# A transformer layer's first stage: value weights loaded ahead of key weights, key weights folded once, 128-row products for the first two pairs of tiles, and a new order of issue

## The chip, the cores and the metric

One core of a Trainium2 chip runs the kernel. The metric is device time in microseconds; the kernel before took 389.91 (median of 3 runs, 389.55 to 390.11). A core has TensorE (PE; its weight loads are shown as PEld), VectorE (DVE), ScalarE (ACT) and GpSimd (POOL), and SyncE (SP), which here only issues transfers. Each takes its instructions in program order; between engines they wait on semaphores. Times inside the execution are from one profiled execution, in us from the start of its span.

## What is computed

2,048 rows of 576 numbers pass a pre-norm layer: linear attention with learned feature maps (32 heads of 18), then an MLP (576 to 4,608 to 576).

```python
x = A_x
y = layernorm(x)
q, k, v = split(y @ wqkv)                      # 32 heads of 18
pq, pk = q @ w_phi, k @ w_phi                  # per head, 18 x 18
phi_q = concat(softmax(pq), softmax(-pq))      # 36 features per head
phi_k = concat(softmax(pk), softmax(-pk))
kv, z = sum_s phi_k v, sum_s phi_k
o = (phi_q @ kv) / (phi_q @ z + 1e-6)
h = x + o @ wo
out = h + gelu(layernorm(h) @ w1 + b1) @ w2 + b2
```

## The kernel before

The 2,048 rows are 16 tiles of 128, worked on as 8 pairs `p` of two tiles. All activations and weights are bf16, products gather in PSUM in fp32.

**Stage one** needs every row before it ends, because `kv` and `z` are sums over all rows. First w_phi is multiplied into the key and query weights ("folding"), so that one product gives `pk` or `pq`. For the keys, the weights (`wk`) are loaded, turned on PE (`flip_mm`, 5 groups of heads, 25 transposes), copied out of PSUM (`flip_ev`), and multiplied by the block-diagonal w_phi `bd` (`fold_k_mm`) into nine blocks of rows `wkp`; `fold_k_ev` copies each block out. The query weights come turned by DMA (`turn_wq`), are folded into five blocks, and the other rows of `wqp` are filled by copies inside SBUF (`swap_q`).

Rows are normalised (`stats`, `power`, `centre`, `scale`) and turned, pair 0 on PE, the others by transposing DMAs on SP (`turn_dma`), into `turned(p)`: 9 blocks of 64 columns of each of the two tiles, tile 0 on partitions 0 to 63 and tile 1 on 64 to 127. A product (`value_mm`, `key_mm`, `query_mm`; line L450) of one pair and one half of the columns is therefore 18 matmuls of 64 rows, in nine couples of one for each tile, that run side by side on the two halves of the array; a pair takes two products, 36 matmuls. There are 16 products of each kind (8 pairs, two halves of 288 columns). ACT copies values out (`value_ev`, L460) and takes the exponentials of keys and queries (two activations each, L472); DVE sums and inverts (`key_sum`, L501 and L503); POOL, sometimes DVE, multiplies (`key_weigh`, L507; `query_weigh`, L536). `sums` (L586) adds a tile's 11 products into `acc_kv`.

Then `table` makes kvm from `acc_kv`, `combine_mm` and `divide` (L686, L687) give o of pair 0, `turn_o_mm` turns it, `residual_mm` (L722) multiplies by wo, DVE adds and normalises (`residual_add`, `second`, `rescale`), and `turn2_mm` turns the rows for **stage two**, the MLP: `up` (L1161, followed by gelu on ACT, L1183) and `down` (L1205), with the attention of later pairs between. Query products that are left fill PE while DVE works on this chain. `gelu_table` (L781) runs one gelu on four numbers ahead of time, so that ACT's table of functions is loaded early.

**Order.** Each engine's order is written out by hand, as one list of calls from `warm(13)` on. Transfers wait in SP's queue (a few in ACT's and POOL's) in the order of the list. PSUM has three tiles of two banks (`two`) for everything in stage one; each call takes the next in turn. After stage one the same banks become six of one bank each (`acc`).

## Time and profile before

| | |
|---|---|
| runs, median (lowest to highest) | 389.91 us (389.55 to 390.11) |
| the profiled execution's span | 391.7 us |
| first value product starts | 15.69 us |
| last of the sums over all rows ends | 66.96 us |
| first MLP product starts | 86.00 us |
| last MLP product ends | 389.03 us |
| weight loads on the chain ahead of the first PE work | 5.99 us |

The profile gives no time of its own for the profiled execution beside its span; the span is 1.8 us longer than the median of the runs. How to read its lines: busy time is the time in which an engine has an instruction running, so 98% on PE does not say that PE runs at its best; "idle" names what released the engine; "issue" is waiting for which the profile shows no cause. The chain of work is followed back from the last instruction to whatever released each step.

### The profile page before, as it was taken

How to read it: one execution, taken by the hardware profiler on the slowest of the kernel's cores; microseconds unless marked ns; L12 is line 12 of the kernel's file. 1: busy time of each engine (PE TensorE's matmuls, PEld its weight loads, DVE VectorE, ACT ScalarE, POOL GpSimd, SP SyncE). 2: the span in 40 equal slices, each digit the busy share in tenths (PEclk: the TensorE clock that was granted, in tenths of full speed). 3: DMA queues.
4: the chain of work that ended last, by engine and by line, in shares of the span. 5: the costliest groups of instructions: out<-in, count | busy, mean ns of one | idle time of the engine just before them, and what ended most of it. 6: DMA issues, size and time to landing. Idle time of an engine off the chain costs nothing.

```text
span 391.7 us, 10190 instructions
## 1 busy us (share of the span) xinstructions
PE 383.0 (98%) x4475; PEld 269.0 (69%) x4475; DVE 166.0 (42%) x364; ACT 163.2 (42%) x291; POOL 117.8 (30%) x161
## 2 busy tenths in 40 slices
PE   7999999799999999999999999999999999999997
PEld 3778779479978887844457887444677764447773
DVE  6998997385249388590019322000480000000100
ACT  2998995478500850046650000666300016661000
POOL 6399998116404654144003111000031110000120
PEclk9999999899999999999999999999999999999999
DMA  8977599999455578433003462000071000000000
GB/s 250 259 128 128 93 218 188 238 313 248 148 105 102 98 105 136 94 66 68 2 2 62 89 108 48 17 1 2 2 105 47 17 15 2 2 2 0 17 28 19
DMA packets 74096, 34.93 MB, mean 89 GB/s; under 512 B 61028, under 2 KB 71524, under 8 KB 74052
## 3 DMA queue, kind: packets, MB, share of 16 engines
q1 hardware_dynamic: 72944, 32.78, 40.3%
q0 software_dynamic: 336, 1.33, 1.2%
q8 instruction: 35, 0.57, 0.7%
q10 hardware_dynamic: 772, 0.17, 0.2%
q14 instruction: 9, 0.07, 0.1%
HBM read 16.47 MB, written 2.36 MB: 48 GB/s over the span
## 4 chain that ended last, share of the span: by engine, by line
PE 93%; ACT 2%; DMA 2%; issue 1%; DVE 1%; SPq 0%
PE po L1205 36%; PE ph L1161 36%; PE pk L450 8%; PE pv L450 5%; PE pa L722 4%; DMA w<-in_A_wqkv_dram 2%; PE acc_kv L586 1%; PE pn L673 1%; ACT home L472 1%; ACT shared L412 0%; DVE xh L731 0%; PE pW L419 0%; PE pW L405 0%; PE pT L359 0%; PE pX L377 0%
## 5 line engine op out<-in xcount | busy, mean ns | idle before, releaser
L1183 ACT ACTIVATE home<-ph,b1col 128x512 bf16<-128x512 f32 (+1 forms) x180 | 98.4, 598 | 169.1 <-PE ph L1161 165.9
L1205 PE MATMUL po<-w,home 128*128 128x288 bf16 (+2 forms) x1152 | 143.3, 286 | 0.0
L1161 PE MATMUL ph<-shared,w 64*128 64x512 bf16 (+2 forms) x1638 | 141.3, 331 | 0.6 <-ACT shared L364 0.6
L1205 PEld LDWEIGHTS <-home 128*128 128x128 bf16 x1152 | 109.4, 98 | 32.1 <-issue 1.8
L1161 PEld LDWEIGHTS <-w 64*128 64x128 bf16 x1638 | 80.3, 94 | 60.5 <-issue 0.7
L1209 DVE TENSOR_TENSOR ot<-po,hb 128x288 bf16<-128x288 f32 (+2 forms) x32 | 14.4, 453 | 106.4 <-PE po L1205 96.7
L450 PEld LDWEIGHTS <-home 64*128 64x128 bf16 x864 | 42.9, 95 | 13.6 <-issue 3.3
L1194 POOL TENSOR_TENSOR hb<-xh,b2bc 128x576 f32<-128x576 bf16 x16 | 20.4, 1273 | 104.6 <-DVE ot L1209 102.8
L536 POOL TENSOR_TENSOR padded<-home,rq 128x540 bf16<-128x540 bf16 x32 | 34.9, 1102 | 34.5 <-DVE rq L528 18.9
L731 DVE TENSOR_TENSOR xh<-pa,xh 128x288 bf16<-128x288 f32 x32 | 13.0, 447 | 72.4 <-PE pa L722 72.4
L274 POOL TENSOR_TENSOR rs<-va,mhalf 128x1 f32<-128x1 f32 x16 | 8.8, 549 | 110.9 <-DVE va L272 110.9
L507 POOL TENSOR_TENSOR phik<-phik,rk 128x576 bf16<-128x576 bf16 x28 | 33.4, 1218 | 1.4 <-DVE rk L503 1.2
L472 ACT ACTIVATE home<-pk 128x576 bf16<-128x576 f32 x32 | 18.6, 665 | 12.7 <-PE pk L450 10.4
L450 PE MATMUL pk<-wqp,home 64*128 64x288 bf16 x288 | 20.5, 293 | 2.8 <-issue 2.8
L501 DVE TENSOR_REDUCE sk<-phik 128x64 f32<-128x1152 bf16 x16 | 21.0, 1312 | 1.7 <-ACT phik L472 1.6
L527 DVE TENSOR_REDUCE sk<-home 128x64 f32<-128x1152 bf16 x16 | 21.0, 1310 | 0.0
L686 DVE RECIPROCAL rec<-pn 128x18 f32<-128x18 f32 (+1 forms) x32 | 8.0, 249 | 28.5 <-PE pn L673 28.5
L450 PE MATMUL pv<-wv,home 64*128 64x288 bf16 x288 | 19.6, 283 | 0.0
L472 ACT ACTIVATE phik<-pk 128x576 bf16<-128x576 f32 x32 | 18.7, 656 | 1.8 <-PE pk L450 1.1
L450 PE MATMUL pk<-shared,home 64*128 64x288 bf16 x288 | 19.3, 283 | 0.0
L722 PE MATMUL pa<-wo,shared 64*128 64x288 bf16 x288 | 18.6, 283 | 0.0
L722 PEld LDWEIGHTS <-shared 64*128 64x128 bf16 x288 | 13.9, 94 | 4.5 <-issue 0.5
(76 smaller groups left out, 208.3 us busy)
## 6 DMA issues: line engine op xcount, KB each, us to landing
w<-in_B_w_dram SPq DMA_DIRECT2D x21, 432.0 KB, 8.7
out_dram<-ot SPq DMA_DIRECT2D x15, 144.0 KB, 2.2
xh<-in_A_x_dram SPq DMA_DIRECT2D x3, 576.0 KB, 6.8
wo<-in_A_wo_dram SPq DMA_DIRECT2D x4, 324.0 KB, 8.0
w<-in_B_w_dram POOLq DMA_DIRECT2D x3, 432.0 KB, 13.0
wv<-in_A_wqkv_dram SPq DMA_DIRECT2D x2, 576.0 KB, 8.7
w<-in_A_wqkv_dram SPq DMA_DIRECT2D x1, 576.0 KB, 6.0
wqp<-wqp SPq DMA_DIRECT2D x2, 288.0 KB, 3.9
```

Source lines behind the costliest of these rows:

```text
L450: nc.tensor.matmul(dst[:, a, 0:HALF], lhs[rows, c, :], w[rows, slot, i * HALF : (i + 1) * HALF], start=(n == 0), stop=(n == KC - 1),)
L472: nc.scalar.activation(rows[:, :, i * HH : (i + 1) * HH, s, :], flight[key, p, i][:, :, 0:HALF].rearrange("p a (h f) -> p a h f", f=DH), A ...
L501: nc.vector.tensor_reduce(sk[:, :, :], part_of(dst, i), AX.X, ALU.add)
L507: eng.tensor_tensor(part, part, flight["r" + key, p, i][:, a, :].rearrange("p (h o) -> p h o", o=1).to_broadcast([P, NH, DH]), ALU.mult,)
L527: nc.vector.tensor_reduce(sk[:, :, :], part_of(phiq[p], i), AX.X, ALU.add)
L536: eng.tensor_tensor(padded[:, a, g0 * P : (g0 + 5) * P].rearrange("p (g k) -> p g k", k=P)[:, :, 0:STEP].rearrange("p g (h f) -> p g h f", ...
L722: nc.tensor.matmul(pa[a], oT[p % 2][rows, c, :], wo[rows, c, cs], start=(c == 0), stop=(c == KC - 1),)
L1161: nc.tensor.matmul(ph[half][:, lo:hi], w1[p_ // 9][rows, c, p_ % 9 * P : (p_ % 9 + 1) * P], ln2T[rows, c, base + lo : base + hi], start=(c ...
L1183: nc.scalar.activation(hidden(m), ph[half][:, 0:width], AF.Gelu_apprx_tanh, bias=b1col[:, m : m + 1], scale=1.0,)
L1194: nc.gpsimd.tensor_tensor(hb[:, :], xh[:, t, :], b2bc[:, :], ALU.add)
L1205: nc.tensor.matmul(po[:, :], hidden(m)[:, i_ * P : (i_ + 1) * P], w2[m // 18][:, m % 18, cs], start=(j == 0), stop=(j == NM - 1),)
L1209: nc.vector.tensor_tensor(ot[:, cs], po[:, :], hb[:, cs], ALU.add)
```

## The change

What it does, by parts:

- **Loads.** The value weights are loaded first, in five pieces; the key weights follow x's tiles 2 and 3. The last 64 rows of the key weights are loaded twice, into both halves of their block. x comes in smaller pieces; wo in two loads in place of four, since `divide` now writes o in an order that makes wo's rows contiguous. The second quarter of w1 is loaded piece by piece in the list, in place of six loads at `close_keys`.
- **Pairs 0 and 1** (`NAT = 2`) keep their rows as they are: `turn_n_mm` turns them on PE into 4 blocks of 128 columns and one of 64 for each tile. Their value, key and query products (`project_n`) are for each tile 8 matmuls of 128 rows and 2 of 64 rows (the "tail"). What follows goes by tiles, not by halves of the columns.
- **Key fold.** Five blocks of 128 rows in place of nine; the odd blocks, which the 64-row products of pairs 2 to 7 need, are copied inside SBUF by two DMAs (`swap_k`).
- **PSUM tiles** are named by number and taken from a list of free ones (`grab`, `give`), in place of pools that hand them out in turn.
- **Order.** The list is new from its first call to the MLP. The first products are pair 0's values.

```diff
-    wTk = borrowed(NG, D).rearrange("p (g f) -> p g f", g=NG)
+    wTk = borrowed(NG, DP).rearrange("p (g f) -> p g f", g=NG)
...
+    def grab(kind, key, shape, dt):
+        n = held[kind, key] = free[kind].pop(0)
...
-    def fold_k_mm(n):
...
     def fold_mm(name, c):
-        m = P if c < NC - 1 else 64
-        flight[name, c] = two.tile([P, 2, 512], FP32, name="pW", tag="two")[:, :, :]
+        flight[name, c] = grab("two", ("fold", name, c), [P, 2, 512], FP32)[:, :, :]
+        src = wTk if name == "k" else wTq
+        f0 = c * P if c < 4 or name == "k" else 448
         for g in range(NG):
             k = P if g < NG - 1 else 72
             nc.tensor.matmul(
-                folded_part(g, name, c, slice(0, m)),
-                wTq[:k, g, c * P : c * P + m],
+                folded_part(g, name, c), src[:k, g, f0 : f0 + P],
...
+    def swap_k(part):
+        if part:
+            nc.sync.dma_start(wkp[KH:P, 1:8:2, :], wkp[0:KH, 0:8:2, :])
+        else:
+            nc.sync.dma_start(wkp[0:KH, 1:8:2, :], wkp[KH:P, 0:8:2, :])
...
+    def project_n(key, p, a, w, slots, tail):
+        if (key, p, a) not in flight:
+            flight[key, p, a] = grab("two", (key, p, a), [P, 2, 512], FP32)[:, :, :]
+            begun[key, p, a] = 0
+        begun[key, p, a] += 1
+        dst, done = flight[key, p, a], begun[key, p, a]
+        steps = [(slice(a * KH, (a + 1) * KH), 8, tail)] if tail is not None else [
+            (slice(0, P), 4 * a + n, slots[n]) for n in range(4)
+        ]
+        for k, (rows, block, slot) in enumerate(steps):
+            for i in range(2):
+                yield (
+                    dst[:, i, 0:HALF], turned(p)[rows, block, :],
+                    w[rows, slot, i * HALF : (i + 1) * HALF],
...
-    def load_wo(part):
...
+    def load_wo(half, eng):
+        eng.dma_start(
+            wo[half * KH : (half + 1) * KH, :, :], A_wo.rearrange("(k c) f -> k c f", c=KC)
         )
...
-        for n in range(6):
-            load_w1(1, n, (nc.sync, nc.gpsimd)[n % 2])
...
+    gelu_table()
+    query_exp(5, 0)
```

Where the list moves instructions, three places matter. The first is SP's queue at the program's start; the rows name line, kind and tile (`xh` is x, `wv` the value weights, `w` with L166 and L168 the key weights, `home` a turned pair). Before:

```order
L192 DMA xh<-in_A_x_dram 128x576
L192 DMA xh<-in_A_x_dram 128x1152
L166 DMA w_0_108<-in_A_wqkv_dram 64x576
L168 DMA w_0_108<-in_A_wqkv_dram 128x4x576
L192 DMA xh<-in_A_x_dram 128x2304 x2
L177 DMA wv<-in_A_wqkv_dram 128x4x576
L185 DMA wv<-in_A_wqkv_dram 64x576
L177 DMA wv<-in_A_wqkv_dram 128x4x576
```

Now, at the same place (the key weights are at L168 and L170):

```order
L193 DMA xh<-in_A_x_dram 128x576
L180 DMA wv<-in_A_wqkv_dram 128x4x576
L188 DMA wv<-in_A_wqkv_dram 64x576
L180 DMA wv<-in_A_wqkv_dram 128x576
L193 DMA xh<-in_A_x_dram 128x1152
L168 DMA w_0_108<-in_A_wqkv_dram 64x576
L170 DMA w_0_108<-in_A_wqkv_dram 128x4x576
L168 DMA w_0_108<-in_A_wqkv_dram 64x576
```

Five and a half of the nine blocks of the value weights have moved ahead of x's second load and of the key weights.

The second is ACT from its first scaling on (`home` is a turned pair, `w` the turned key weights, the casts into `shared` the folded ones, `vals` values). Before:

```order
L290 ACTIVATE shared<-xh,nb,rs 128x9x64
L383 COPY w_0_108<-pX 128x576
L290 ACTIVATE shared<-xh,nb,rs 128x9x64
L383 COPY w_0_108<-pX 128x576
L364 COPY home_63<-pT 128x512
L412 CAST shared<-pW 128x576 x7
L290 ACTIVATE shared<-xh,nb,rs 128x9x64
L412 CAST shared<-pW 128x576
```

Now:

```order
L309 ACTIVATE shared<-xh,nb,rs 128x576
L413 COPY home_63<-two_195 128x640
L519 CAST vals<-two_207 128x32x18
L519 CAST vals<-two_233 128x32x18
L426 COPY w_0_108<-two_250 128x640
L426 COPY w_0_108<-two_264 128x640
L426 COPY w_0_108<-two_272 128x640
L426 COPY w_0_108<-two_278 72x640
L413 COPY home_63<-two_295 128x640
L453 CAST shared<-two_304 128x576
L453 CAST shared<-two_315 128x576
```

Pair 0's values are copied out first, ACT takes four of the five turned groups where it took two, and five fold copies follow (two are shown) where it made eight.

The third is ACT where stage two begins: the last exponentials of the queries (`home` from PSUM, two activations each), the copy of the turned rows (`shared`), the one gelu on `spare`, and the first gelus of the MLP. Before:

```order
L472 ACTIVATE home_70<-pk 128x2x16x18 x2
L472 ACTIVATE home_67<-pk 128x2x16x18 x2
L364 COPY shared<-pT 128x4x128
L781 ACT_TABLE_LOAD
L781 ACTIVATE spare<-mhalf 128x4
L1183 ACTIVATE home_63<-ph,b1col 128x256
```

Now:

```order
L543 ACTIVATE home_71<-two_1775 128x2x16x18 x2
L385 COPY shared<-two_1819 128x4x128
L926 ACT_TABLE_LOAD
L926 ACTIVATE spare<-mhalf 128x4
L543 ACT_TABLE_LOAD
L543 ACTIVATE home_68<-two_1798 128x2x16x18 x2
L1343 ACT_TABLE_LOAD
L1343 ACTIVATE home_63<-acc_1872,b1col 128x256
```

One pair of exponentials has moved behind the copy and behind the gelu on `spare`, and the program holds three table loads where it held one.

More of the change, by code (lines that the diff above doesn't have):

```diff
@@ L112 @@
     two = psA.enter_context(
-        tc.tile_pool(name="two", bufs=3, space=bass.MemoryType.PSUM, reuse_waits="tile")
+        tc.tile_pool(name="two", bufs=1, space=bass.MemoryType.PSUM, reuse_waits="tile")
     )
@@ L354, in transposes @@
             parts = [
-                two.tile([P, 5 - e, P], BF16, name="pT", tag="two")[:, :, :] for e in range(2)
+                grab("two", (key, e), [P, 5 - e, P], BF16)[:, :, :] for e in range(2)
             ]
@@ L364, in turned_back @@
         copy(dst[:, 5 * part : 5 + 4 * part, :], flight[key][part])
+        give("two", (key, part))
     def turn_x_mm(p):
@@ L580, in sums @@
         left.remove(t)
+        last = t + 1 - 2 * a not in left
         for w in range(KW):
@@ new lines @@
+    key_sum(3, 0)
+    load_w1(0, 1, syn)
+    query_n_sum(0, 1)
+    load_wo(1, syn)
+    value_mm(5, 1)
+    value_ev(5, 1, act)
+    key_weigh(5, 1, 1, pool)
+    key_weigh(3, 0, 1, vec)
+    turn_dma(7)
+    key_mm(7, 0)
+    scale(6, 1, act)
+    key_exp(7, 0)
+    key_sum(7, 0)
+    key_weigh(4, 0, 0, pool)
+    key_mm(5, 0)
+    value_mm(5, 0)
+    value_ev(5, 0, act)
+    key_exp(5, 0)
+    sums(4, 0)
+    sums(2, 1)
+    sums(4, 1)
+    key_mm(7, 1)
+    value_mm(7, 0)
+    value_ev(7, 0, act)
```

824 lines of the change are left out of this document (458 added, 366 removed).

## The prediction

> **What bounds the kernel now.** I read the page first (busy shares and the clock row), then the stretches of 10 us, then the chain that ended last, and last the order of time at the places that the chain names.
>
> ```profile
> PE 383.0 (98%) x4475; PEld 269.0 (69%) x4475; DVE 166.0 (42%) x364; ACT 163.2 (42%) x291; POOL 117.8 (30%) x161
> PEclk9999999899999999999999999999999999999999
> ```
> ```profile
> 0.00:10.00 10.00, 7.66 (x49) 3.96 (x49) 6.37 (x19) 2.96 (x5) 6.28 (x26) 1.00 0.82 253
> ...
> 30.00:40.00 10.00, 10.00 (x191) 8.23 (x187) 8.81 (x16) 9.04 (x16) 9.42 (x14) 1.00 0.62 132
> ...
> 70.00:80.00 10.00, 7.23 (x91) 5.00 (x89) 3.73 (x11) 3.58 (x6) 0.00 (x0) 0.83 1.05 252
> ```
> ```profile
> 2.32 5.99 DMA w<-in_A_wqkv_dram
> ...
> 15.69 2.31 PE pv L450 x36
> 18.00 4.41 PE pk L450 x72
> ...
> 37.45 2.20 PE pv L450 x36
> ...
> 63.71 3.25 PE acc_kv L586 x110
> 66.96 1.21 PE pk L450 x18
> ...
> 70.60 2.77 issue
> ...
> 81.02 3.19 ACT home L472 x6
> ...
> 86.00 17.88 PE ph L1161 x342
> ```
> TensorE is the bound: from 15.69 us on the chain is PE almost without a break. So a change gains only by letting PE's useful work begin earlier, by taking work off PE, or by closing a hole; whatever opens a hole costs its whole length. The one large hole before the MLP is at 70.60, and the one stretch with a lower clock is the same (0.83). In the first 67 us ACT, DVE and POOL are nearly as full as PE (30 to 40: 9.04, 8.81, 9.42 of 10), so PE's start alone does not set when this stage ends. I call the end of the last sum, 66.96, T.
>
> **Part 1, the start: about 0.1 us.** The value weights now go ahead of the key weights.
>
> ```profile
> 8.36 2.41 PE L377 MATMUL pX<-ident,w 128*128 128x128 bf16 x25 [0.92 <-DMA w<-in_A_wqkv_dram]
> ...
> 9.39 0.64 ACT L383 COPY w<-pX 128x576 bf16<-128x576 bf16 x1 [0.77 <-PE pX L377]
> ...
> 11.41 0.58 ACT L364 COPY home<-pT 128x512 bf16<-128x512 bf16 x1
> ...
> 11.97 4.02 ACT L412 CAST shared<-pW 128x576 bf16<-128x576 f32 x7
> ...
> 15.87 0.89 ACT L290 ACTIVATE shared<-xh,nb,rs 128x576 bf16<-128x576 bf16 x1
> ```
> ```profile
> 20.37 1.35 DVE L501 TENSOR_REDUCE sk<-phik 128x64 f32<-128x1152 bf16 x1
> ...
> 21.76 0.55 DVE L503 RECIPROCAL rk<-sk 128x64 f32<-128x64 f32 x1
> ...
> 22.46 2.28 POOL L507 TENSOR_TENSOR phik<-phik,rk 128x576 bf16<-128x576 bf16 x2
> ...
> 25.76 1.19 ACT L472 ACTIVATE phik<-pk 128x576 bf16<-128x576 f32 x2 [0.27 <-PE pk L450]
> ```
> ```profile
> 62.71 3.31 POOL L507 TENSOR_TENSOR phik<-phik,rk 128x576 bf16<-128x576 bf16 x2
> ```
> The key weights land at 2.32 + 5.99 = 8.31. Ahead of them now stand 0.81 MB of value weights (128 x 576 x 2 bytes x 4 blocks, one more block, and half a block). The first 10 us move 253 GB/s, nothing of it before about 2.3 us, so 0.33 MB per us while loads run: 2.45 us later, 10.75. Bounds: 0 (transfers share the engines, and the order costs nothing) to 3.2 (at 253). Meanwhile PE does pair 0's values. Then, back to back on ACT: the first flip (2.41/5 = 0.5), four flip copies of 0.64, one transposed copy of 0.58, five fold copies of 4.02/7 = 0.57, which ends at 17.2; the key product may start after the third fold copy, 16.1. Before, keys began at 18.00, also with two value products behind them. PE is thus 1.9 us ahead: half the folds are gone (25 of 50 products) and nine fold copies are five.
>
> But POOL does not start ahead. Behind the folds on ACT come one scaling (0.89) and two pairs of exponentials (1.19 each): 20.5; then DVE's sum and reciprocal, 1.9: first weighing at 22.4, against 22.46. From there to its last weighing (62.71 + 3.31 = 66.02) POOL has the same 28 weighings and four query weighings as before, and it was 92 to 95% busy. PE's own sum gives T = 16.1 + (66.96 - 15.69) - 2.20 (two value products already done) + 0.6 = 65.8, which POOL's chain covers. **T moves by -0.1**; bounds -2 (POOL's idle, some 0.6 us in every 10, all used) and +1.5 (weights at the slow end, and ACT and PE handing three PSUM tiles to and fro).
>
> The 0.6: 128-row products for pairs 0 and 1 change nothing by themselves (16 full ones and 4 half-row tails take the place of 36 half-row ones; below, 288 full ones of 288 columns take 35.40, 0.123 each, and 36 half-row ones 2.20, so 2.2 either way). But a group that follows full-row work took 2.31, not 2.20: 0.11 per entry, about six more entries.
>
> ```profile
> 353.62 35.40 PE po L1205 x288
> ```
> Edits at nothing, each with its cover: two SBUF copies for the odd key blocks (like wqp's, 3.9 us) are issued at 17.2 and needed by the first half-row key product, after some 8 us of other products, near 25; behind them on SP wait pair 2's transposing DMA (3.6) and the last x loads, needed near 25 and 31. The query weights' three transposes (4.3) are issued by 14.2, needed at 19.5. If a cover fails, up to 1.5 us, which is T's upper bound. Two wo loads in place of four, the other order inside ob and the hand-numbered PSUM tiles keep their durations.
>
> ```profile
> wqp<-wqp SPq DMA_DIRECT2D x2, 288.0 KB, 3.9
> ...
> home<-shared SPq DMA_TRANSPOSE x7, 3.6
> ...
> w<-in_A_wqkv_dram SPq DMA_TRANSPOSE x3, 4.3
> ```
>
> **Part 2, the hole at 70.60: -3.3 us.**
>
> ```profile
> 71.23 0.42 DVE L687 TENSOR_TENSOR ob<-pn,rec 128x252 bf16<-128x252 f32 x1
> 73.37 0.86 PE L450 MATMUL pk<-wqp,home 64*128 64x288 bf16 x10 [2.77 <-issue]
> 74.16 1.14 PE L359 MATMUL pT<-ident,ob 128*128 128x128 bf16 x9
> ```
> ```profile
> 74.00:76.00 2.00, 2.00 (x21) 1.39 (x19) 0.66 (x2) 1.19 (x2) 0.00 (x0) 0.50 1.03 243
> 76.00:78.00 2.00, 2.00 (x26) 1.36 (x24) 0.16 (x1) 0.42 (x1) 0.00 (x0) 0.66 1.05 289
> ```
> ```profile
> q1 hardware_dynamic: 557, 1.03, 103.7%
> q8 instruction: 1, 0.02, 1.7%
> ```
> PE stops in the middle of a product, on nothing that it waits for by name ("issue"), and in just these 5 us (69 to 74) one instruction block arrives while the data queue fills all 16 engines (103.7%). I read this as PE out of instructions: 110 short sums had used them up quickly, behind a burst of weight loads. The transposes of o, ready at 71.65 (last divide), began at 74.16: 2.5 lost; then the clock at 0.50 and 0.66 lost 1.0 + 0.7. Together 4.2. In the changed kernel PE has 228 rows fewer ahead, so the block boundary falls elsewhere, and the loads before T come earlier. But the profiled span, 391.7, is 1.8 above the median of the runs, 389.91 (what lies around the span would only add to this), and this hole is the one irregular thing in the trace. If all of that is a longer hole, the runs hold 2.4. I take the middle, 3.3; ends 2.4 and 4.2.
>
> **Part 3, the last exponentials behind the table load: -0.65 and +3.1 us.**
>
> ```profile
> 82.68 2.01 DVE L278 TENSOR_SCALAR shared<-xh,mv,rs 128x576 bf16<-128x576 bf16 x4 [0.39 <-POOL rs L274]
> ...
> 85.33 0.62 ACT L364 COPY shared<-pT 128x512 bf16<-128x512 bf16 x1
> ...
> 85.97 1.28 ACT L781 ACT_TABLE_LOAD   x1
> ...
> 87.26 0.20 ACT L781 ACTIVATE spare<-mhalf 128x4 f32<-128x4 f32 x1
> 87.37 2.63 ACT L1183 ACTIVATE home<-ph,b1col 128x256 bf16<-128x256 f32 x6
> ```
> gelu's table is now loaded before the last query exponentials, so the program holds three loads there: gelu, exp, gelu. The exponentials (1.19) no longer stand ahead of the copy at 85.33; DVE's rescaling ends at 84.69 and the copy can follow its transposes near 84.7, so the first MLP product comes 0.65 earlier (bounds 0 and 1.19). But from the copy's end to the first gelu ACT takes 1.28 + 0.20 + 1.28 + 1.19 + 1.28 = 5.2, where it took 1.4. PE needs 17.88/18 = 0.99 per pair of MLP rows and has PSUM for three pairs: the fourth would start 2.98 after the first and needs the first pair's two gelus (2.63/6 = 0.44 each) done, at 5.2 + 0.88 = 6.1. **A hole of 3.1 us**, in two pieces of about 1.9 and 1.2, since the third pair's banks are those that the late exponentials read. Nothing covers it; bounds 2.4 (ACT done early) and 3.8 (the whole delay).
>
> The Trainium skill ("ScalarE: Activation LUTs", Table sets: the hidden batching unit) says to do all calls of one table set together, which speaks against this edit, and the trace has exactly one load there. Its section on what ACT_TABLE_LOAD costs counts a drain of some 1.38 us with each; by that the estimate would be two drains, some 2.8 us, longer. Here the next instruction starts at 87.26, 0.01 behind the load, so I leave the drain out.
>
> **Sum** on the profiled execution: 391.7 - 0.1 - 4.2 - 0.65 + 3.1 = 389.85. For the runs, with the smaller hole: 389.91 - 0.1 - 3.3 - 0.65 + 3.1 = **389.0**, own range 388.1 to 389.9.
>
> **The rivals.**
> *The start gains as well*: POOL's idle shrinks and T comes 1.0 earlier, and the hole was worth 4.2 in the runs: 389.0 - 1.0 - 0.9 = 387.1. For it: PE has 1.9 us in hand. Against: three engines over 88% busy. Chance 0.20.
> *The new hole costs clock* (the other side): a hole of 2.77 brought 0.50 for some 3.4 us; the new one leaves PE 3.1 us idle with one pair between. If that counts as one hole, half of 3.4 us is lost: 389.0 + 1.7 = 390.7. It decides from how much PE works in between: 0.92 us of idle at 7.4 left the clock at 1.00. Chance 0.18. The Trainium skill ("TensorE: Matmul & The Clock Gate", Part 1) gives an idle window of about 3.4 us, by which neither piece would do it; but by that rule the hole of 2.77 should not have done it alone either, and it did.
> *The missing block moves, not goes*: at T the burst of loads starts as before, and a block boundary falls some 11 us later, in the last query products ahead of the MLP, where PE has nothing in hand: 2.77 more, 391.8. For it: that burst filled the engines to 103.7% for this long. Against: a block asked for at T has some 10 us to come. Chance 0.18.
> *Each table load drains ACT* for as long as it lasts: 2 x 1.28 = 2.6 more, 391.6. The 0.01 above speaks against it. Chance 0.05. This is the skill's drain as a mechanism here.
> *The start is late* by its upper bound, 1.5: 390.5. Chance 0.09.
>
> **How the numbers follow.** The forecast has 0.30. I call faster or slower what differs by over 0.2%, 0.78 us, about what a measurement of this kernel can tell. Faster: 0.17 of the forecast's 0.30 and all 0.20 of the first rival, 0.37. Same: 0.13 of the forecast, 0.10 of the clock's 0.18, 0.02 of the block, 0.04 of the late start, 0.29. Slower: 0.08 + 0.16 + 0.05 + 0.05 = 0.34. The range, 386.6 to 392.2, reaches past the first rival by half a us and past the moved block by 0.4; what is left out are two mishaps together, or both good ends.
>
> **What would show it.** Step 1: pair 0's value products end near 10.3, key weights land near 10.7, first weighing near 22.4, last sum within 1.5 us of 66.9. Step 2: no hole marked "issue" over 1 us between the last sum and the first MLP product, some 14 us in place of 19.04, the clock at 1.00. Step 3: three table loads, the first gelu 5.2 behind the copy, PE idle for 3 us there with ACT named. The forecast is wrong if the last sum moves by over 2 us, if "issue" holds PE again, or if the clock falls after the new hole.

## The result: 1.4% slower, and the profile after

The changed kernel takes 395.86 us (median of 4 runs, 393.87 to 396.12) against 389.88 (389.55 to 390.11) for the kernel before on the same chip: ratio 1.0142, 95% interval 1.0113 to 1.0170. The forecast was 389.0, its range ended at 392.2.

The page of the changed kernel, busy time of the engines and the granted clock in 40 slices:

```profile
PE 385.7 (98%) x4361; PEld 267.1 (68%) x4361; DVE 167.6 (43%) x362; ACT 165.4 (42%) x292; POOL 117.2 (30%) x162
PEclk9999999998999999999999999999999999999999
```

PE has 114 products fewer and is busy 2.7 us longer; the one slice with a lower clock has moved from the eighth to the tenth, behind the start of the MLP. The chain that ended last in the changed kernel (start, length, what; pieces of under 0.2 us are left out):

```profile
20.87 1.44 PE two L506 x12
...
22.57 0.98 PE two L506 x8
...
50.83 4.19 DVE exk L611
...
66.92 1.97 PE acc_kv L723 x61
...
82.61 0.58 ACT shared L385
83.21 1.28 ACT L926
84.71 1.28 ACT L543
86.01 1.19 ACT home L543 x2
87.22 1.28 ACT L1343
88.52 0.85 ACT home L1343 x2
89.40 16.51 PE acc L1321 x269
105.92 0.35 PE acc L1366 x2
```

The last sum now ends at 66.92 + 1.97 = 68.89 (T), where it ended at 66.96. Behind the copy at 82.61 stand the three table loads of 1.28 (at L926, L543, L1343), and PE's down products start at 105.9. PE's own rows show the waits, in brackets with what ended them:

```profile
83.24 2.28 PE L1321 MATMUL acc<-shared,w 64*128 64x128 bf16 x54
87.25 1.16 PE L1321 MATMUL acc<-shared,w 64*128 64x256 bf16 x18 [1.73 <-ACT home L543]
89.04 1.37 PE L1321 MATMUL acc<-shared,w 64*128 64x256 bf16 x8 [0.63 <-ACT home L1343]
```

And the stretch of 4 us in which the second of these waits ends (the number ahead of DMA share and GB/s is the granted clock):

```profile
88.00:92.00 4.00, 3.27 (x35) 2.39 (x33) 3.27 (x4) 3.47 (x9) 2.83 (x5) 0.67 1.55 307
```

From the starts and ends of PE's rows, five profiles by stage, in us (the second profiles and the kernel with one table load are told of below):

| | before, first profile | before, second | changed, first | changed, second | one table load |
|---|---|---|---|---|---|
| T, last sum ends | 66.96 | 66.50 | 68.89 | 68.70 | 67.99 |
| T to the first MLP product | 19.04 | 15.61 | 14.35 | 14.80 | 14.52 |
| from there to the first down product | 17.82 | 17.99 | 22.61 | 20.99 | 18.36 |
| from there to the end of the last product | 285.19 | 285.19 | 285.92 | 285.92 | 285.93 |
| span | 391.7 | 388.0 | 394.4 | 393.0 | 389.4 |
| time of this execution | not known | 389.74 | 396.12 | 394.76 | 391.14 |

Where both are known, the time is 1.7 to 1.8 above the span. The four runs of the changed kernel at 396.12, 396.01, 395.70 and 393.87 had a mean clock of 0.996, 0.996, 0.996 and 1.000: the last one did not pay for the lower clock. The loss of that one stretch, 0.33 of 4 us and 0.09 of the next 4, is what half the clock for some 3.4 us would cost; it is called the half clock below.

### The profile page after: what moved, and what is told of

It reads as the page before. It is cut to its first block, busy times and chain, and to the rows that moved or that the text cites. A ratio compares the mean times of both kernels' runs of the same rounds, so it can differ in the third digit from the quotient of the medians.

```text
span 394.4 us, 9972 instructions
## 1 busy us (share of the span) xinstructions
PE 385.7 (98%) x4361; PEld 267.1 (68%) x4361; DVE 167.6 (43%) x362; ACT 165.4 (42%) x292; POOL 117.2 (30%) x162
## 4 chain that ended last, share of the span: by engine, by line
PE 86%; DVE 7%; ACT 4%; POOL 1%; issue 1%; POOLq 0%; DVEq 0%; ACTq 0%
PE acc L1366 36%; PE acc L1321 35%; PE acc L863 4%; PE two L506 3%; PE two L480 3%; DVE sk L605 3%; PE two L286 1%; DVE rk L607 1%; DVE ob L827 1%; DVE exk L611 1%; POOL exk L611 1%; ACT exk L543 1%; PE acc_kv L723 1%; ACT w L426 1%; PE pn L813 1%
## 5 line engine op out<-in xcount | busy, mean ns | idle before, releaser
L1343 ACT ACTIVATE home<-acc,b1col 128x512 bf16<-128x512 f32 (+1 forms) x180 | 98.2, 598 | 170.9 <-PE acc L1321 168.2
L1321 PE MATMUL acc<-shared,w 64*128 64x512 bf16 (+2 forms) x1638 | 144.1, 334 | 2.8 <-ACT home L543 1.7
L1366 PE MATMUL acc<-w,home 128*128 128x288 bf16 (+2 forms) x1152 | 143.3, 286 | 0.0
L1370 DVE TENSOR_TENSOR ot<-acc,hb 128x288 bf16<-128x288 f32 (+2 forms) x32 | 14.5, 452 | 106.1 <-PE acc L1366 100.4
L611 POOL TENSOR_TENSOR exk<-exk,rk 128x576 bf16<-128x576 bf16 x20 | 24.1, 1233 | 3.7 <-DVE rk L607 3.7
L543 ACT ACTIVATE home<-two 128x576 bf16<-128x576 f32 x24 | 13.8, 661 | 8.3 <-PE two L480 8.3
L297 DVE TENSOR_SCALAR shared<-xh,mv,rs 128x576 bf16<-128x576 bf16 x32 | 16.2, 567 | 0.6 <-POOL rs L293 0.4
L863 PE MATMUL acc<-wo,shared 64*128 64x288 bf16 x252 | 16.4, 283 | 0.0
L605 DVE TENSOR_REDUCE sk<-exk 128x64 f32<-128x1152 bf16 x12 | 15.8, 1317 | 0.2 <-ACT exk L543 0.2
L480 PE MATMUL two<-wv,home 64*128 64x288 bf16 x216 | 14.9, 283 | 0.0
L480 PE MATMUL two<-wqp,home 64*128 64x288 bf16 x216 | 14.6, 283 | 0.1
```

The costliest lines, as they stand in the source:

```text
L297: nc.vector.tensor_scalar(dst, src, mv[:, i, 0:1], rs[:, i : i + 1], ALU.subtract, ALU.mult)
L480: nc.tensor.matmul(dst[:, a, 0:HALF], lhs[rows, c, :], w[rows, slot, i * HALF : (i + 1) * HALF], start=(n == 0), stop=(n == KC - 1),)
L543: nc.scalar.activation(rows[:, :, i * HH : (i + 1) * HH, s, :], flight[key, p, i][:, :, 0:HALF].rearrange("p a (h f) -> p a h f", f=DH), A ...
L605: nc.vector.tensor_reduce(sk[:, :, :], part_of(dst, i), AX.X, ALU.add)
L611: eng.tensor_tensor(part, part, flight["r" + key, p, i][:, a, :].rearrange("p (h o) -> p h o", o=1).to_broadcast([P, NH, DH]), ALU.mult,)
L863: nc.tensor.matmul(pa[a], oT[p % 2][rows, c, :], wo[rows, c, cs], start=(c == 0), stop=(c == KC - 1),)
```

## The experiments

Ratios are to the kernel before on the same chip, with the 95% interval; chips differ by up to 0.3% in the kernel before (389.23 to 390.39).

### Was the hole at 70.60 in the runs? The kernel before, unchanged

> The kernel before, unchanged, for a second profiled execution. Theory (the hole of 2.77 us at 70.60 and the half clock behind it, 4.2 us together, belong to the one profiled execution and not to the timed runs): the span that goes with a time of 389.9 is near 388, that is 1.8 below the time, and if this profile shows that span, it has no stop marked issue over 1 us between the last sum and the first MLP product, which then are 14.5 to 15.5 us apart. Rival (the hole is in every run, as the prediction had it): the profile shows it again, 18 to 19 us from the last sum to the first MLP product, and a span near 391.7.

389.96 us (10 runs), 0.9991 (0.9977 to 1.0005); the profiled execution took 389.74 with a span of 388.0. PE's rows:

```profile
63.18 3.32 PE L586 MATMUL acc_kv<-vals,phik 128*128 128x57 bf16 x110
...
70.47 0.79 PE L450 MATMUL pk<-wqp,home 64*128 64x288 bf16 x10 [0.34 <-issue]
...
82.11 1.11 PE L1161 MATMUL ph<-shared,w 64*128 64x128 bf16 x33 [0.71 <-ACT shared L364]
```

At the place of the 2.77 there are 0.34, the clock stays at 1.00, and T is 15.61 ahead of the first MLP product, 0.1 more than expected. The theory holds: the profiled execution of before was an odd one. Not one of 10 runs here and 22 beside it took longer than 391.35, and a span of 391.7 means some 393.4. An instruction block arrives here too, between 67 and 68 us; in the first profile one arrived between 70 and 71. A late block as the cause of the 2.77 would fit that, but two profiles do not show it.

### One table load

```diff
-    gelu_table()
     query_exp(5, 0)
+    gelu_table()
```

> The changed kernel with the last query exponentials ahead of the load of gelu's table, so that there is one table load instead of three. Theory (the three loads cost PE 3.1 us of waiting, and the half clock that follows costs 1.7 more in most runs): 4.3 to 4.8 us less than the changed kernel's 395.9, so 391.1 to 391.6, a granted clock of 1.00 from 86 to 94 us, 17.9 to 18.5 us from the first to the last product of the first MLP block's first half in place of 22.7. Rival A (the clock falls for another reason, the start of the MLP itself): 3.1 less, 392.8, and half clock still there. Rival B (PE would have waited anyway, for weights or for the copy): less than 1 us less, 395 or more.

391.36 us (11 runs), 1.0027 (1.0018 to 1.0036), 4.5 below the changed kernel. ACT's rows, and the clock in the stretch that had 0.67:

```profile
81.88 0.59 ACT L385 COPY shared<-two 128x512 bf16<-128x512 bf16 x1 [0.51 <-PE two L380]
82.36 1.20 ACT L543 ACTIVATE home<-two 128x576 bf16<-128x576 f32 x2
83.58 1.28 ACT L926 ACT_TABLE_LOAD   x1
...
84.98 4.94 ACT L1343 ACTIVATE home<-acc,b1col 128x256 bf16<-128x256 f32 x12
```
```profile
88.00:92.00 4.00, 4.00 (x78) 3.56 (x74) 2.38 (x4) 3.36 (x8) 1.94 (x3) 1.00 1.25 265
```

The first gelu starts 2.5 behind the copy, PE does not wait, the clock is 1.00 in all 11 runs, and the first MLP stage falls from 22.61 to 18.36. As expected, with hole and clock; both rivals fall. Of the 5.0 between the two spans 4.25 lie in this stage, and 0.9 in T, ahead of the table loads; 0.6 of these stand at the first key product already (16.20 against 16.80).

### The same edit alone, in the kernel before

```diff
-    query_exp(1, 0)
     rescale(0, 1)
...
     gelu_table()
+    query_exp(1, 0)
     load_w2(0, 0)
```

> The kernel before with its last query exponentials moved behind the load of gelu's table: part 3 of the change alone. Theory: 3.1 - 0.65 for the hole and 1.7 for the clock, so 2.5 to 4.2 us more than the kernel before, 392.4 to 394.1. Rival (what was lost was lost to the start and not here): within 0.8 of 389.9.

395.71 us (4 runs), 1.0152 (1.0126 to 1.0178): 5.3 more, above the expected end. PE waits once and longer than in the changed kernel, since here the first pair of MLP rows already needs banks that the late exponentials read; the clock in the stretch is 0.51:

```profile
85.82 4.56 PE L1161 MATMUL ph<-shared,w 64*128 64x128 bf16 x58 [3.81 <-ACT home L472]
```
```profile
84.00:88.00 4.00, 2.18 (x39) 2.18 (x40) 2.17 (x3) 1.86 (x4) 0.12 (x1) 0.51 1.09 357
```

All four runs show a lower mean clock (0.991 to 0.995), and none of the 22 runs of the kernel before beside them does (0.999 or more). So this edit alone costs as much as the whole change. The first MLP product comes 15.04 behind T here, 0.57 sooner than in the second profile of before: that is part 3's -0.65.

### Hole or clock: PE kept at work in the first hole

```diff
-            pair(ph, p_, P if p_ < first else 0, width)
+            for _ in range(3 if (p0, p_) == (0, 1) else 1):
+                pair(ph, p_, P if p_ < first else 0, width)
```

> The changed kernel, with the second pair of MLP rows of the first block computed three times over (two more times 18 products, about 2.0 us of PE work, nothing else changed), so that PE works through the first piece of the hole behind the table loads (1.73 us) instead of standing still; ACT and its three loads stay. Theory (the half clock there comes from PE's standing still): the clock stays at 1.00 from 86 to 94 us, the hole that is left is at most 0.6, the up stage takes 21.0 to 21.3 us in place of 22.7, and the time is 1.4 to 2.1 below the changed kernel's 395.9: 393.8 to 394.5. Rival (the clock falls whatever PE does there, and the 1.73 are lost anyway): 395.5 or more.

393.82 us (4 runs), 1.0116 (1.0090 to 1.0142), clock 0.999 to 1.000 in all. The stretch that had 0.67:

```profile
88.00:92.00 4.00, 3.84 (x67) 3.66 (x68) 2.17 (x3) 3.86 (x12) 1.70 (x3) 1.00 1.31 244
```

ACT still loads three tables, PE does 2 us of work that nobody needs, and the first MLP stage takes 20.98 in place of 22.61. All this is as expected, but it does not show that the filled hole kept the clock up: the changed kernel's repeat, told of below, has its holes open, keeps its clock at 1.00 all the same, and takes 20.99 for this stage. The time does not show it either, since 1.0116 is not told apart from 1.0142, and T is 67.74 in this profile against 68.89. That standing still can cost the clock rests on the experiment before this one, with 3.81 us of waiting: a lower clock in four of four runs, against none of 22.

### DVE's long weighing, given to POOL

```diff
     query_weigh(0, 1, 1, pool)
+    key_weigh(3, 0, 1, pool)
...
-    key_weigh(3, 0, 1, vec)
```

> The changed kernel with one weighing, that of pair 3, columns 0, tile 1, taken from DVE (4.19 us there, at 50.83) to POOL behind its two query weighings, where POOL idles 2.63 us. Theory (that weighing holds DVE until POOL's queue runs dry, DVE's sums behind it come 3 to 4 us late, and PE waits 0.18 at 53.6 and 0.74 at 66.18 for what follows from them): the DVE weighing is gone, those two holes close, the last sum ends at 67.6 to 68.2 in place of 68.89, and the time is 0.7 to 1.2 us less, 394.7 to 395.2. Rival (PE's own work sets the end of the sums, and the holes move elsewhere): the last sum stays within 0.3 of 68.89 and the time within 0.4 of 395.9.

394.95 us (4 runs from 393.44 to 397.59), 1.0126 (1.0093 to 1.0160). T stays at 68.85: the next weighing on DVE, of pair 7, takes 4.38 in its place, and the holes are 0.28, 0.46 and 0.38. That is what the rival expected, but it decides nothing, since what was to be removed came back at another place; the clock differs between its runs too (0.991 to 1.000).

### o's old order

```diff
-        o = ob[t // 2 % 2][:, :, t % 2, :].rearrange("p c (h e) -> p c e h", e=2)
+        o = ob[t // 2 % 2][:, :, t % 2, :].rearrange("p c (e h) -> p c e h", e=2)
...
-                pv[:, :, 0:DH].rearrange("p h (e c) -> p c e h", e=2),
+                pv[:, :, 0:DH].rearrange("p h (c e) -> p c e h", e=2),
```

> The run with one table load (391.36), with the order of o's columns and the four loads of wo as they were before the change. Theory (between the first down stage and the end the changed kernel loses 0.74 us, all of it at one place, where PE waits 0.34 and a weight load 0.22 for a PSUM bank that the slower divides give back late; the new order makes the 128x324 divide 0.57 in place of 0.50 and the 128x252 one 0.48 in place of 0.42): 0.5 to 0.75 less, 390.6 to 390.9, and no hole near 137 us. Rival (the hole comes from the new order of PSUM banks and not from o's order): the divides are shorter, the hole stays, within 0.2 of 391.36.

391.61 us (6 runs), 1.0053 (1.0035 to 1.0072). With one table load PE waits here, ahead of a pair of MLP rows (the 71 products):

```profile
137.62 4.10 PE L1321 MATMUL acc<-shared,w 64*128 64x256 bf16 x71 [0.34 <-DVE ob L827]
```

With o's old order, PE, and one of DVE's divides:

```profile
137.84 4.10 PE L1323 MATMUL acc<-shared,w 64*128 64x256 bf16 x71 [0.33 <-DVE ob L829]
```
```profile
136.68 0.50 DVE L829 TENSOR_TENSOR ob<-acc,rec 128x324 bf16<-128x324 f32 x1
```

The divide is back at 0.50 and the hole stays at 0.33; the last stretch is 285.79 in place of 285.93. So the divides account for 0.14 of the 0.74. My theory fell for the rest; its rival (the numbering of PSUM banks) is left, and a run below tests it.

### Key weights first

```diff
+    load_wk(2, syn)
+    load_wk(0, syn)
+    load_wk(1, syn)
-    load_values(0, syn)
-    load_values(2, syn)
-    load_values(1, syn)
...
     fold_ev("k", 4, act)
+    value_n_mm(0, 0)
...
```

> The run with one table load (391.36), with the key weights' loads ahead of the value weights' (the two groups change places) and pair 0's value products behind the key fold: the loads of part 1 undone, the single fold, the copies and the 128-row products kept. Theory (PE's work from the first key product on, 51.8 us in that run, sets the last sum, so T moves with the start): key weights land near 8 instead of 10.6, the folds' copies end near 14.8, pair 0's values take 2.5 of PE behind them, the first key product starts at 15.4 to 16.0 instead of 16.2, T is 67.2 to 67.8 instead of 67.99, and the time 0.2 to 0.8 less, 390.6 to 391.2. Rival A (the value products in hand were worth their 2.2 us): T 1.5 to 2.2 later, 392.9 to 393.6. Rival B (POOL's chain, which ends its weighings at 65.6, sets T): T within 0.2.

392.63 us (4 runs), 1.0080 (1.0060 to 1.0100). PE's first key product, and its last sums:

```profile
17.59 0.78 PE L506 MATMUL two<-shared,home 128*128 128x288 bf16 x5
```
```profile
67.58 1.98 PE L723 MATMUL acc_kv<-vals,exk 128*128 128x57 bf16 x61 [0.68 <-POOL exk L611]
```

The flips begin at 8.32 instead of 10.63, but ACT's last fold copy ends at 16.21, only 1.0 earlier, and then pair 0's values take their 2.4: keys start at 17.59, 1.39 later, and T is 69.56, 1.57 later. Rival A comes nearest. In four other profiles with one table load and the value weights first (the run above and its repeat, o's old order, the other bank), keys start at 16.20 to 16.69 and T is 67.99 to 68.72, so loading the value weights first is worth some 0.8 to 1.6 us to this order.

### Other waits closed

```diff
-    load_w1(0, 2, syn)
     turn_dma(5)
+    load_w1(0, 2, syn)
...
     turn_dma(7)
+    load_w1(0, 1, syn)
+    load_wo(1, syn)
```

On the kernel with o's old order; two groups of fillers are left out as well.

> The kernel with one table load and the old order of o, with three more edits of order that only close waits of PE before T: one group of 4 filler products behind the first key products and one in the key fold left out, and two transposing transfers (pairs 5 and 7) issued ahead of the w1 and wo loads in front of them on SP's queue. Theory (PE's work sets the end everywhere, so each closed hole pays in full): 0.47 and 0.26 for the two waits on transfers and 0.2 to 0.3 for the fillers, so 0.7 to 1.0 below the run with the old order of o: 389.7 to 390.1 if that is 390.7, that is at or below the kernel before. Rival (DVE and POOL set T): T within 0.3 of 67.99 and the time within 0.3 of the run with the old order of o.

394.03 us (6 runs), 1.0119 (1.0093 to 1.0145). A miss: the transposing transfer of pair 7 waits in SP's queue for the copy of a value product, and the w1 and wo loads behind it then run in front of pair 6's:

```profile
34.37 9.01 SPq L363 DMA_TRANSPOSE home<-shared  x2
43.43 0.88 SPq L754 DMA_DIRECT2D w<-in_B_w_dram  x1
44.36 1.29 SPq L767 DMA_DIRECT2D wo<-in_A_wo_dram  x2
```
```profile
57.73 2.54 PE L480 MATMUL two<-shared,home 64*128 64x288 bf16 x22 [4.51 <-DMA home<-shared]
```

The two waits (0.58 and 0.33 in the kernel with o's old order) became one of 4.51. In this queue a transfer that had to wait held up what stood behind it. Four of the six runs show a mean clock of 0.996.

### The changed kernel again

> The changed kernel, unchanged, on one chip with the three kernels beside it. Theory (T, the last sum, is 1.4 to 2.4 later than before, the table loads and the clock cost 4.3 to 4.8, PE's waits between the last sum and the first MLP product are 1.1 shorter, and the PSUM banks cost 0.6 to 0.75): ratio to the kernel before 1.012 to 1.017; the profile shows three table loads, two holes of together 2.1 to 2.6 us behind the first MLP products, T between 67.7 and 69.0. Rival (the 1.4% were of one chip only): ratio below 1.010.

394.07 us (4 runs, 393.57 to 394.76), 1.0095 (1.0076 to 1.0113): below the expected ratio, and even the rival's line is only just met. The three loads and the holes are there, and yet:

```profile
87.51 1.16 PE L1321 MATMUL acc<-shared,w 64*128 64x256 bf16 x18 [1.85 <-ACT home L543]
89.30 0.96 PE L1321 MATMUL acc<-shared,w 64*128 64x256 bf16 x8 [0.63 <-ACT home L1343]
```
```profile
88.00:92.00 4.00, 3.27 (x58) 2.90 (x55) 3.36 (x4) 3.99 (x10) 2.93 (x5) 1.00 1.41 312
```

The clock stays at 1.00, in this run and in the other three. The same holes went with a lower clock in three of four executions on one chip and in none of four on this one; in the run with the weighing on POOL, which has the three loads too, in two of four. So part of the change's loss comes and goes: 1.0095 without the half clock, 1.0142 with it in most runs. Whether the chip or chance decides is not shown.

### The other PSUM bank

```diff
+            13: other_bank,          # swaps entries 3 and 4 of free["acc"]
```

> The changed kernel with one table load, and with two entries of the list of free PSUM banks changed about once, ahead of pair 13 of the MLP rows in the second block: pair 14 then takes only one of the two banks that the combine's product has just used, as in the kernel before, and pair 15 the other. Theory (the 0.74 us that the changed kernel loses at 137 us are PE's waits for these two banks): no hole there, first down stage to the end 285.2 to 285.4 in place of 285.93, and the time 0.5 to 0.75 below the run with one table load (1.0027 of the kernel before): 1.0006 to 1.0016. Rival (the wait is for o's divides and only moves to another bank): a hole of 0.2 or more stays between 135 and 142 us.

391.09 us (11 runs), 1.0025 (1.0011 to 1.0038). PE's row at the place:

```profile
135.22 6.19 PE L1321 MATMUL acc<-shared,w 64*128 64x256 bf16 x108
```

No wait, although the 128x324 divides still take 0.57: the last stretch is 285.31, 0.6 less. The theory holds at its place. The time, 1.0025, missed the expected 1.0006 to 1.0016 and is no lower than that of the run with one table load (1.0027); in its profile T is 68.66 in place of 67.99, which takes back what the bank gives. What T was in the other runs is not known.

### One transfer ahead and fewer fillers

```diff
-    filler(4)
...
-    load_w1(0, 2, syn)
     turn_dma(5)
+    load_w1(0, 2, syn)
```

> As the kernel beside it (one table load, the other bank), with the transposing transfer of pair 5 issued ahead of one w1 load on SP's queue and one group of 4 filler products behind the first key products left out. Theory (PE's work and its waits set the last sum): PE's wait of 0.3 to 0.6 at 37.5 closes and 0.2 goes with the fillers, so the stretch from the first key product to T is 51.0 to 51.4 us in place of 51.8, and the time 0.3 to 0.8 below the kernel beside it. Rival (a wait for POOL's or DVE's last weighings takes their place): that stretch stays within 0.2 of 51.8.

390.47 us (12 runs), 1.0005 (0.9991 to 1.0018). The wait at 37.5 closes, but PE waits 0.61 at 46.4 for another transfer and 0.43 ahead of the last sums for POOL: first key product to T 52.11. That is the rival's mechanism, at 0.3 above 51.8. The time is 0.6 below the kernel beside it, as the theory had it, but the two intervals overlap.

### The new order of the tail, in the kernel before

```diff
     query_mm(7, 1)
     table(0)
+    combine_mm(1, 0, two)
     table(1)
...
     turn2_ev(0, 0, dve)
+    query_exp(1, 0)
     gelu_table()
```

> The kernel before up to the last sum, and from there to the MLP the changed kernel's order of products, copies and exponentials (the same eight query products stand in the places that the changed kernel gives to its eight), with one table load behind the last exponentials. Theory (what the change wins is the 1.1 us between the last sum and the first MLP product, 15.61 before and 14.52 with the new order, less 0.37 that the last exponentials behind the copy cost in the up stage): 14.4 to 14.8 from the last sum to the first MLP product, and 0.4 to 0.9 us below the kernel before, ratio 0.9977 to 0.9990. Rival (the waits there come from the pairs themselves, or the stop marked issue, and not from the order): within 0.2 us of the kernel before.

392.13 us (9 runs), 1.0068 (1.0043 to 1.0092). T to the first MLP product is 15.90, no better than 15.61; PE stands still for the normalised rows instead:

```profile
81.86 0.68 PE L359 MATMUL pT<-ident,shared 128*128 128x128 bf16 x9 [1.56 <-DVE shared L278]
```

So the shorter tail of the changed kernel is not got by its order of calls alone, as the rival had it. The time is 1.8 above the kernel before, which neither expected. In this profile that loss lies behind the tail, where PE waits for the second MLP weights; from the first down product to the end it takes 287.01 in place of 285.19:

```profile
105.54 0.90 PE L1205 MATMUL po<-w,home 128*128 128x288 bf16 x6 [1.20 <-DMA w<-in_B_w_dram]
```

Two of the nine runs, 395.17 and 395.58, also show a lower clock (0.996 and 0.991).

### What sets T: PE's work or the weighings

```diff
-        both = [list(project_n(key, p, a, w, None, tails[a])) for a in range(2)]
-        multiply(step for pair in zip(*both) for step in pair)
+        for a in range(2):
+            list(project_n(key, p, a, w, None, tails[a]))
```

> The changed kernel with one table load, and without the tails of pairs 0 and 1: the last 64 of the 576 rows are left out of their value, key and query products (24 matmuls, in six groups of four, five of them behind the first key product). Nothing else is left out; the weighings on POOL and DVE are as many as before. Theory (PE's work sets the last sum, and a group of tails costs its own two slots of 0.122 and two changes between 128-row and 64-row work of about 0.1 each): the stretch from the first key product to the last sum is 1.8 to 2.4 us shorter than in the kernel beside it, in which it was 51.3 to 52.1, so 49.3 to 50.1, unless the weighings, whose last ended 2.4 us ahead of the last sum there, become the bound after 1.2 or more. Rival A (a change of form costs nothing, the tails only their slots): 1.2 shorter. Rival B (the weighings on DVE and POOL set the last sum): shorter by less than 0.4.

> The kernel with one table load again, beside the one without tails on the same chip. Both theories: first key product to last sum 51.3 to 52.1 us; ratio to the kernel before 1.0015 to 1.005.

391.20 us (10 runs), 1.0037 (1.0020 to 1.0053) without the tails; 391.48 (4 runs), 1.0046 (1.0029 to 1.0063) beside it. First key product (16.41 and 16.58) to T (68.49 and 68.68): 52.08 and 52.10. PE's work was less, and without the tails PE only waits longer:

```profile
37.84 2.38 PE L480 MATMUL two<-shared,home 64*128 64x288 bf16 x36 [1.08 <-DMA home<-shared]
...
47.36 2.38 PE L480 MATMUL two<-shared,home 64*128 64x288 bf16 x36 [0.52 <-DMA home<-shared]
```

Rival B: here the weighings set T. In both profiles, and in five of the six others in which DVE's weighing at 50 to 52 us takes 3.85 or more (the changed kernel's two among the five), T comes 0.39 to 0.40 behind the end of POOL's last weighing; in the sixth PE is held up by the wait of 4.51. The kernel beside it is the same as in the run with one table load, where that stretch was 51.79 and POOL's last weighing 2.4 ahead of T. What differs first is one instruction, DVE's weighing at 50.8. One table load, first run, DVE and POOL:

```profile
50.77 1.36 DVE L611 TENSOR_TENSOR exk<-exk,rk 128x576 bf16<-128x576 bf16 x1
```
```profile
54.38 4.64 POOL L611 TENSOR_TENSOR exk<-exk,rk 128x576 bf16<-128x576 bf16 x4
59.75 5.85 POOL L611 TENSOR_TENSOR exk<-exk,rk 128x576 bf16<-128x576 bf16 x4 [0.73 <-DVE rk L607]
```

The same kernel, second run:

```profile
50.92 3.89 DVE L611 TENSOR_TENSOR exk<-exk,rk 128x576 bf16<-128x576 bf16 x1
```
```profile
56.83 3.41 POOL L611 TENSOR_TENSOR exk<-exk,rk 128x576 bf16<-128x576 bf16 x3 [2.63 <-DVE rk L607]
...
62.44 5.85 POOL L611 TENSOR_TENSOR exk<-exk,rk 128x576 bf16<-128x576 bf16 x4 [0.73 <-DVE rk L607]
```

With 1.36 POOL ends at 65.60; with 3.89 DVE's next sums are late, POOL idles 2.63 for them, and ends at 68.29.

### The long weighing moved, or given away with the next

```diff
-    key_weigh(3, 0, 1, vec)
...
     key_weigh(5, 0, 1, vec)
+    key_weigh(3, 0, 1, vec)
```

> The kernel with one table load, the other bank and pair 5's transfer ahead (1.0005 of the kernel before), with DVE's weighing of pair 3 moved from 50.3 us to behind DVE's weighing of pair 5, ahead of the last sums. Theory (that weighing waits some 4 us on DVE while POOL works without a pause, and the seven sums behind it on DVE, then POOL's last weighings, come that much later): without it at that place DVE's sums run on, POOL's last weighing ends near 65.5 to 66.5 instead of 68.08, first key product to last sum is 51.0 to 51.7 in place of 52.11, and the time 0.4 to 1.0 us less, ratio 0.998 to 0.9995. Rival (a DVE weighing waits for POOL wherever it stands): one of the four takes 3 us or more, the stretch stays at 52.0 or more, the time within 0.2 us.

> The same kernel, with the weighing of pair 3 and the next one, of pair 7, given to POOL, so that DVE has two weighings left, both at the end. Theory: DVE does not wait in mid-stage, POOL has 2.3 us more work but none of its 3.6 us of idle, its last weighing ends 67.0 to 68.0, the stretch is 51.3 to 52.0. Rival (one of the two that are left waits for POOL): it takes 3 us or more, and the stretch is 52.3 or more.

Moved: 390.17 us (12 runs), 1.0012 (1.0001 to 1.0022). The two weighings that now stand together on DVE, and POOL's last four:

```profile
61.55 2.56 DVE L611 TENSOR_TENSOR exk<-exk,rk 128x576 bf16<-128x576 bf16 x2
```
```profile
59.28 5.85 POOL L611 TENSOR_TENSOR exk<-exk,rk 128x576 bf16<-128x576 bf16 x4 [0.73 <-DVE rk L607]
```

POOL ends at 65.13, and the stretch to T is 51.57: the theory holds in the profile, while the time missed the expected 0.998 to 0.9995 and is not told apart from the kernel that it started from (1.0005). Both given to POOL: 390.56 us (12 runs), 1.0015 (1.0007 to 1.0023); POOL's ten weighings in one piece, and DVE:

```profile
53.80 11.26 POOL L611 TENSOR_TENSOR exk<-exk,rk 128x576 bf16<-128x576 bf16 x10
```
```profile
61.23 4.43 DVE L611 TENSOR_TENSOR exk<-exk,rk 128x576 bf16<-128x576 bf16 x1
```

One of the two that DVE has left waits 4.43, until POOL's run ends at 65.05; the stretch is 52.07. It is the rival's mechanism, with less harm than it named. No version beats the kernel before: the best, 1.0005 and 1.0012, equal it to within 0.2%.

## Why the prediction was wrong, by its steps

**Part 2, "-3.3 for the hole at 70.60", is the step that failed most.** The hole was there in one profiled execution; in the second it was 0.34. What made it 2.77 in the first stays open. The text had the clue: the span was 1.8 above the runs' median and "what lies around the span would only add to this". It adds 1.7, so that execution was some 3.5 us longer than the runs, and of the 4.2 no more than 0.7 was to be had. I used 2.4 as the lower end. What the change did win between T and the first MLP product is 15.61 - 14.80 = 0.8 (second profiles) to 1.3, part of it the 0.65 that part 3 had counted for itself.

**Part 1, "T moves by -0.1", came out at +1.9 in the first profile and +2.2 between the second ones.** Its start was about right: the first key product starts at 16.80 and 16.60 in the changed kernel's two profiles and at 16.20 with one table load (predicted 16.1), where the flips begin at 10.63 (10.75). Two bounds were mis-sized, and both lie near T. *PE's own sum*, 49.7 from the first key product, is 51.3 to 52.0 in the four profiles in which the last weighings end 2 us or more ahead of T (51.57 in the run with the weighing moved). PE's waits were put at nothing: in that run 0.24 for exponentials of the keys and 0.33 and 0.23 for two transposing transfers, 0.8 together. And a group of 64-row tails costs more than its slots: the chain of the changed kernel has 0.98 for 8 full products and 1.44 for 12 entries, so 0.46 for four tails that fill two slots of 0.12, and 0.22 for the two changes of form. If all five groups are alike, that is 1.1, where I had 0.66. Some 0.6 of the 1.9 stays without a name.

*The weighings*: the first on POOL starts at 24.00 instead of 22.4, and with DVE's weighing at 4.19 the last ends at 68.50 instead of 66.0. The changed kernel's rows at the start:

```profile
18.48 2.28 ACT L570 ACTIVATE exk<-two 128x576 bf16<-128x576 f32 x4
...
21.04 0.77 DVE L331 BATCH_NORM_STATS2 st<-xh 128x6 f32<-128x288 bf16 x2
...
21.96 1.30 DVE L627 TENSOR_REDUCE sk<-exk 128x64 f32<-128x1152 bf16 x1
...
24.00 9.00 POOL L636 TENSOR_TENSOR exk<-exk,rk 128x576 bf16<-128x576 bf16 x8 [0.41 <-DVE rk L632]
```

ACT's exponentials end at 20.76 (20.5 predicted), but DVE's sum does not follow at once, as the prediction had it: DVE is at the statistics of later tiles until then, and takes the sum 1.2 later. The prediction also took DVE's weighings as work of fixed length. In the profile of before the four stand together ahead of the last sums; in the new order one stands in the middle of a long run of POOL's.

**Part 3, "-0.65 and +3.1", was right in mechanism and near in size.** Three loads, first gelu 5.3 behind the copy (5.2 predicted); the stage is 3.0 longer without the clock (20.99 against 17.99). The two holes themselves are 1.73 and 0.63, where 1.9 and 1.2 were forecast.

**The rival "the new hole costs clock", +1.7 at a chance of 0.18, came true in its mechanism on the first chip:** 22.61 against 20.99 is 1.6. On another chip it did not. The Trainium skill ("TensorE: Matmul & The Clock Gate", Part 1) describes a free-running window of about 3.4 us and has the clock fall after an idle window of that length. That a hole sometimes counts and sometimes doesn't agrees with a window that runs freely; that holes of 1.73 and 0.63 count at all does not agree with the idle window's length, and here the measurement decides. With longer holes the half clock came more often: 2.77 in the one profile that has it, and in the kernels whose profiles show 3.81 and 4.51 a lower clock in four of four and four of six runs.

The rivals of the moved block and of the draining table loads did not come true: between T and the first MLP product no stop marked "issue" is over 0.3 in the changed kernel's two profiles, and ACT's next instruction stands 0.01 to 0.02 behind each load.

**"Keep their durations" for the hand-numbered PSUM tiles missed 0.73**, all of it at one place (at 142.6 in the changed kernel's first profile, at 137.6 with one table load): pair 14 of the MLP rows takes both banks that the combine's product has just used. One swap of two entries takes 0.6 of it back.

The sum by the second profiles: +2.2 - 0.8 + 3.0 + 0.7 = 5.1, and the spans differ by 5.0 (the medians by 3.8: that profiled execution was the longest of its four). On the first chip the clock adds 1.6 in three of four runs; the medians there differ by 6.0, where this sum would give 6.7.

What stays open: why the same DVE weighing takes 1.4 in one execution and 4 in another; what of the 1.2 us between the second profiles' 5.0 and the medians' 3.8 is chance in T; and what decides whether the short holes cost the clock.

## What to carry to other kernels

Before a hole of a profile is credited, compare the profiled execution with the runs: its time, not its span, and a second profile if the difference is as large as the hole. An activation that was moved across a table load cost two more loads here and what the engine behind it stood still for, and that stand-still could cost the clock as well. Where two engines end a stage within a microsecond of each other, closing a hole of one bought nothing here: both have to be summed with their waits.

## What the runs showed that I had not expected

A weighing on DVE (two inputs in SBUF) that is issued while POOL works through weighings without a pause took either about 1.4 us (1.36, 1.41, 1.35) or 3.85 to 4.43 (ten profiles: pair 3's at 50 to 52 us in eight, another at 59 to 62 in two), and at these places nothing between; the shortest on DVE took 0.69. In the long cases it ends 0.6 after POOL's run, four or five of POOL's instructions later (55.02 and 54.41 in the changed kernel). In the three short ones it ends 0.6 after the one POOL instruction that was running, and POOL's next takes 1.6 in place of 1.1. The Trainium skill ("SBUF — State Buffer", Who interferes with whom) says that a DVE instruction with two SBUF inputs contends with a GpSimd instruction that reads SBUF, and that the port pair that they share is an exclusive lock. The trace agrees that one waits for the other, but in the long cases the wait is for a whole run of instructions and not for one.
